# Linear attention and a two-layer MLP on one core: batch 2 projected five groups sooner, its q transposed behind its keys, w_out groups of batch 1's block moved

## The chip, the cores and the metric

The kernel runs on one core of a Trainium2 chip. The metric is device time in microseconds (us) for one execution.

## The reference

For each of 8 batches and 8 heads, keys and values of 1024 tokens are projected to 64 rows, and every query attends to those 64. The result (8192 tokens of 512) goes through two layers with a hard-swish between them.

```python
def _attn_ref(q, k, v, E, F):
    k_proj = np.einsum('ks,bhsd->bhkd', E, k)
    v_proj = np.einsum('ks,bhsd->bhkd', F, v)
    scores = scale * np.matmul(q, k_proj.transpose(0, 1, 3, 2))
    ...                                        # softmax over the 64 projected keys
    return np.matmul(attn, v_proj)

def _moe_ref(x, w_in, w_out):                  # (8192, 512), (512, 2048), (2048, 512)
    h = x @ w_in
    g = h * np.clip(h + 3.0, 0.0, 6.0) / 6.0
    return g @ w_out
```

## The kernel before

The two layers of batch b run while the attention of batch b+1 is fitted in between ("block" below is the loop body of one b). A block has two halves t of 512 tokens; each half has 16 w_in groups (`first_group`, index `fo`). In between stand four `second_group`s, each a quarter of the w_out product of the half before. The stages of the next batch's attention are hung on those w_out groups by the table `plan`.

```python
        if b == 1:
            plan = {4: (4, second.all_scores), 5: (3, second.all_sums), 6: (2, second.first_values),
                    7: (2, lambda: second.some_values((2, 3), ((pmm, pmm), (pmm, pat))))}
        # ... other batches
        for t in range(NB):                    # NB = 2
            g = g_tile()
            for fo in range(FO):               # FO = 16
                # ... the w_in group fo (the first two of a block together)
                pop()                          # one small deferred action, if any
                if b == 1 and t == 0 and fo == 10:
                    second.projected()         # keys and values of batch 2 projected
                if not behind or fo % SB < SB - 1:     # SB = 4: after groups 3, 7, 11, 15
                    continue
                n = t * SB + fo // SB
                if (b, n) == (1, 7):
                    second.first_products()
                when, act = plan.get(n) or (None, None)
                rows = second_group(*behind[0], fo // SB, ...)
                # ... runs in quarters; act() after quarter `when`
            behind = [(b, t, g)]
```

Batch 1 is the first batch that runs in this loop, and `behind` is empty in its first half: its four w_out groups (n = 4 to 7) all stand in the second half, and the whole attention of batch 2 hangs on them. The softmax denominators take a trip through DRAM: ScalarE turns the sums into 16 rows, SyncE writes them to DRAM, and eight transfers, one for each head, read two rows each back to 64 partitions.

```python
        def spread(self, few):
            nc.scalar.activation(few, few, AF.Exp, scale=-1.0)
            rows = dram.tile([H * NB, TOK], f32, tag="rows", name="rows")
            nc.sync.dma_start(out=rows, in_=few[::8])
            # ... recs: four tiles, one for each pair of heads
            for h in range(H):
                (nc.sync, nc.gpsimd)[h % 2].dma_start(out=..., in_=...to_broadcast([D, NB * TOK]))
```

The products `xT = values * rec` (VectorE, two for each pair of heads) make the x that the next block's first w_in group reads. The loads of batch 3 start here, when a tiny GpSimd copy (`mark`) has read what the last transpose wrote:

```python
        def turn(self):
            nc.sync.dma_start_transpose(self.kT, self.kp.rearrange("p h a d -> p (h a d)"))
            last = self.kT[:1, 0, :1]
            if self.b not in (2, 3):
                qT_dma[self.b] = q_transposed(self.b)
                last = qT_dma[self.b][:1, 0, 0, :1]
            if self.b + 1 < B:
                mark = att.tile([1, 1], bf16, tag="mark", name="mark")
                nc.gpsimd.tensor_copy(mark, last)
                load_kqv(self.b + 1, "qkv" if self.b == 2 else "kvq")
```

For batch 2 the transpose of q was issued elsewhere, ahead of batch 1's block and so ahead of the keys' in SyncE's queue.

The softmax here doesn't subtract the row's maximum and nothing guards it: scores larger than these inputs give would overflow.

Of the kernel before, what the change touches and what calls it, by code (L numbers as in the profile page):

```python
# [15 lines left out]
def kernel(  # L16
# [23 lines left out]
    SB = SO // NB  # L40
# [25 lines left out]
    def pmm():  # L66
        return ps_mm.tile([P, TOK], f32, tag="mm", name="mm")
# [5 lines left out]
    def g_tile():  # L73
        return gpool.tile([P, FO, TOK], bf16, tag="g", name="g")
# [48 lines left out]
    def load_kqv(b, order="qkv"):  # L123
        kqv[b] = {}
        for n in order:
            kqv[b][n] = raw_tile(n)
            nc.gpsimd.dma_start(out=kqv[b][n], in_=kqv_dram[n][b])
# [32 lines left out]
    def q_transposed(b):  # L160

        t = qT_pool.tile([P, KO, 2, TOK], bf16, tag="qT", name="qT")
        nc.sync.dma_start_transpose(t.rearrange("p j a (m n) -> p (j a m) n", n=P),
                                    kqv[b]["q"].rearrange("p h s d -> p (h s d)"))
        return t

    qT_dma = {}
# [5 lines left out]
    def in_columns(ps, stationary, moving, **flags):  # L173
        for lo in range(0, stationary.shape[-1], width[0]):
            nc.tensor.matmul(ps[lo:lo + width[0]], stationary[:, lo:lo + width[0]], moving, **flags)  # L175
# [17 lines left out]
    class Attention:  # L193
# [20 lines left out]
            nc.vector.tensor_copy(self.vp[a * KP:(a + 1) * KP], self.ps[KP:].rearrange("p (h d) -> p h d", d=D))  # L214



        def turn(self):
            nc.sync.dma_start_transpose(self.kT, self.kp.rearrange("p h a d -> p (h a d)"))
            last = self.kT[:1, 0, :1]  # L220
            if self.b not in (2, 3):
                qT_dma[self.b] = q_transposed(self.b)
                last = qT_dma[self.b][:1, 0, 0, :1]
            if self.b + 1 < B:
# [3 lines that stand above are left out]
# [285 lines left out]
    def first_group(xT, t, g, fo):  # L513
        h_ps = pmm()
        h_part(h_ps, xT, t, fo, range(KO))
        h_out(h_ps, g, fo)

    def out_rows(b, t, c):
        return out_v[b, :, SB * t + 2 * (c % 2) + c // 2, :]


    def second_group(b, t, g, c, copy=None):
        o_dst = out_rows(b, t, c)
        if (b, t, c) == (B - 1, NB - 1, SB - 1):

            most = d_model * 3 // 4
            for piece, copy, dma in ((slice(0, most), nc.vector.tensor_copy, nc.sync),
                                     (slice(most, d_model), nc.scalar.copy, nc.scalar)):
                n = piece.stop - piece.start
                o_ps = pmm()[:, :n]  # L530
                for fo in range(FO):
                    in_columns(o_ps, g[:, fo, c * P:(c + 1) * P], w_out_sb[:, fo, piece],
                               start=(fo == 0), stop=(fo == FO - 1))
                o_sb = opool.tile([P, d_model], f32, tag="o_sb", name="o_sb")[:, :n]
                copy(o_sb, o_ps)  # L535
                dma.dma_start(out=o_dst[:, piece], in_=o_sb)
            return
        o_ps = pmm()
        for fo in range(FO):
            in_columns(o_ps, g[:, fo, c * P:(c + 1) * P], w_out_sb[:, fo, :],  # L540
                       start=(fo == 0), stop=(fo == FO - 1))
            if fo % SB == SB - 1:
                yield
        o_sb = opool.tile([P, d_model], f32, tag="o_sb", name="o_sb")
        (copy or nc.scalar.copy)(o_sb, o_ps)  # L545
        nc.sync.dma_start(out=o_dst, in_=o_sb)

    def whole(gen):
        for _ in gen:
            pass  # L550

    def x_tile():
        return xpool.tile([P, KO, NB, TOK], bf16, tag="xT", name="xT")
# [42 lines left out]
    behind = []  # L596
# [3 lines left out]
    def pop():  # L600
        if later:
            later.pop(0)()

    rows = [second_group(0, 0, g[0], c) for c in range(SB)]
# [14 lines left out]
    for c in range(SB):  # L619
        for i, _ in enumerate(second_group(0, 1, g[1], c, nc.vector.tensor_copy)):  # L620
# [3 lines left out]
            elif i == 2 or c == SB - 1:  # L624
                while rest:
                    rest.pop()()
    qT_dma[2] = q_transposed(2)
    xT = x_next


# [3 lines left out]
    for b in range(1, B):  # L634
        if b + 1 < B:
            x_next = second.xT = x_tile()
        third = Attention(b + 2) if b + 2 < B else None


        plan = {}  # L640
        two = (pmm, pmm), (pat, pat)
# [3 lines that stand above are left out]
        elif b + 1 < B:  # L645
            plan = {3 + (b == 2): (2, third.projected) if third else None,
                    4 + (b == 2): (2, lambda: second.some_values((0, 1), two)),
                    6: (2, lambda: second.some_values((2, 3), two, third))}
            if b == 2:
                plan.update({0: (2, second.projected), 1: (4, second.all_scores), 2: (4, second.all_sums)})  # L650
            else:
                plan.update({0: (1, lambda: second.some_scores((1, 2, 3), ((pmm, pmm), (pat, pat), (pat, pat)))),
                             1: (4, second.all_sums)})

        for t in range(NB):
            g = g_tile()
            for fo in range(FO):
                if b < 3 and t == 0 and fo < 2:

                    if fo == 0:  # L660
                        TwoGroups(xT, t, g).parts((0, 1, 2), (3,))
                else:
                    first_group(xT, t, g, fo)
                pop()
                if b == 1 and t == 0 and fo == 10:
                    second.projected()
                if not behind or fo % SB < SB - 1:
                    continue
                n = t * SB + fo // SB
                if (b, n) == (1, 7):  # L670
                    second.first_products()
                when, act = plan.get(n) or (None, None)

                rows = second_group(*behind[0], fo // SB,
                                    nc.vector.tensor_copy if second and act == second.all_scores else None)
                for quarter in range(1, SB + 1):
                    next(rows) if quarter < SB else whole(rows)
                    if quarter == when:
                        act()
            behind = [(b, t, g)]  # L680
        if b == 1:
            later.append(lambda: qT_dma.update({3: q_transposed(3)}))
        second, xT = third, x_next
# [32 lines left out]
```

## Time and profile before

| | before |
|---|---|
| time, median (range) of the first 3 runs | 508.66 us (507.2 to 510.09) |
| profiled run: time, span, granted clock | 507.9 us, 505.8 us, 0.999 |
| TensorE busy | 496.9 us (98%) |
| waits of TensorE for x of batch 2 | 1.87 + 0.56 = 2.43 us |

The lines that show this are in the prediction. Two more views are needed for what follows. First the timeline of TensorE and of SyncE's queue around batch 1's block; columns are start in us, duration, engine (PE is TensorE, DVE VectorE, POOL GpSimd, SPq the queue of SyncE), line, operation, output<-input and count; a bracket at the end holds a wait before the line and what ended it. A transfer "lands" when all of its data has arrived; its line in SyncE's queue is over before that (q's transpose below leaves the queue at 97.38 and lands at 99.5). The first line is the start of the block, which is the zero point for comparing profiles, because starts of the program differ by up to 1.5 us between runs (1.3 from before's).

```profile
84.17 9.68 PE L175 MATMUL mm<-xT,w_in_sb 128*32 128x512 bf16 x176
...
92.00 5.38 SPq L163 DMA_TRANSPOSE qT<-q  x1
97.48 1.21 SPq L219 DMA_TRANSPOSE kT<-kp  x1
...
117.52 0.53 SPq L286 DMA_DIRECT2D rows<-few  x1
122.21 2.38 SPq L290 DMA_DIRECT2D rec<-rows  x4
```

The keys' transpose starts at 97.48, right after q's has left the queue, though VectorE had finished its input at 96.94. The rows leave at 117.52 and are back for the broadcasts at 122.2.

Second, busy time by stretches of 1 us; the last three columns are the granted clock of TensorE, the mean busy share of the DMA engines (it can exceed 1: 1.11 in the first line) and GB/s.

```profile
120.00:121.00 1.00, 1.00 (x20) 0.25 (x12) 0.28 (x1) 0.00 (x0) 0.00 (x0) 1.00 1.11 293
...
122.00:123.00 1.00, 1.00 (x24) 0.54 (x20) 0.00 (x0) 0.00 (x0) 0.22 (x1) 1.00 0.02 3
```

Between the end of batch 3's loads and the broadcasts the DMA engines are all but idle for about two microseconds: 3 GB/s in the second line.

### The profile page before, as it was taken

How to read it: one execution, taken by the hardware profiler on the slowest of the kernel's cores; microseconds unless marked ns; L12 is line 12 of the kernel's file. 1: busy time of each engine (PE TensorE's matmuls, PEld its weight loads, DVE VectorE, ACT ScalarE, POOL GpSimd, SP SyncE). 2: the span in 40 equal slices, each digit the busy share in tenths (PEclk: the TensorE clock that was granted, in tenths of full speed). 3: DMA queues.
4: the chain of work that ended last, by engine and by line, in shares of the span. 5: the costliest groups of instructions: out<-in, count | busy, mean ns of one | idle time of the engine just before them, and what ended most of it. 6: DMA issues, size and time to landing. Idle time of an engine off the chain costs nothing.

```text
span 505.8 us, 18693 instructions
## 1 busy us (share of the span) xinstructions
PE 496.9 (98%) x8562; PEld 246.2 (49%) x8562; DVE 245.7 (49%) x384; ACT 244.3 (48%) x425; POOL 51.4 (10%) x82
## 2 busy tenths in 40 slices
PE   8999999999899999999999999999999999999997
PEld 4554554454354444444454544454445444444444
DVE  3572746853744474337533555436552465334420
ACT  3657476565246445633564434652456444443431
POOL 8620020011020120012001020010000100000000
PEclk9999999999999999999999999999999999999999
DMA  9999979799929999469942889257111611101112
GB/s 169 197 205 209 192 146 232 134 161 194 236 53 205 275 148 208 107 189 173 201 100 73 184 156 213 65 138 191 44 43 42 183 55 43 44 23 44 45 44 86
DMA packets 78815, 68.91 MB, mean 136 GB/s; under 512 B 36400, under 2 KB 67376, under 8 KB 78736
## 3 DMA queue, kind: packets, MB, share of 16 engines
q0 software_dynamic: 34400, 35.66, 42.3%
q1 hardware_dynamic: 44112, 31.73, 23.2%
q8 instruction: 67, 1.10, 0.9%
q10 hardware_dynamic: 224, 0.33, 0.3%
q14 instruction: 12, 0.10, 0.1%
HBM read 71.83 MB, written 16.97 MB: 176 GB/s over the span
## 4 chain that ended last, share of the span: by engine, by line
PE 92%; DMA 6%; POOL 1%; issue 1%; ACT 0%; DVE 0%; POOLq 0%; DVEq 0%; ACTq 0%
PE mm L175 85%; PE at L175 2%; DMA rec<-rows 2%; DMA w_in_sb<-in_moe_w_in_dram 2%; DMA k<-in_k_dram 1%; DMA rows<-few 1%; PE mm L254 1%; PE at L236 1%; PE mm L236 1%; PE at L254 1%; PE mm L275 1%; PE at L422 0%; POOL rec L290 0%; POOL q L109 0%; POOL k L113 0%
## 5 line engine op out<-in xcount | busy, mean ns | idle before, releaser
L511 DVE SCALAR_TENSOR_TENSOR g<-r,mm 128x512 bf16<-128x512 f32 x256 | 174.5, 687 | 189.7 <-ACT r L510 189.0
L175 PE MATMUL mm<-w_out_sb,g 128*32 128x512 bf16 (+3 forms) x3904 | 235.9, 376 | 0.0
L175 PE MATMUL mm<-xT,w_in_sb 128*32 128x512 bf16 (+1 forms) x3840 | 231.5, 379 | 2.8 <-DVE xT L267 2.4
L510 ACT ACTIVATE r<-mm 128x512 f32<-128x512 f32 x256 | 153.0, 599 | 74.0 <-PE mm L175 72.0
L175 PEld LDWEIGHTS <-w_in_sb 128*32 128x32 bf16 (+1 forms) x3840 | 110.2, 98 | 113.6 <-issue 4.1
L175 PEld LDWEIGHTS <-g 128*32 128x32 bf16 (+1 forms) x3904 | 109.4, 98 | 111.5 <-issue 6.7
L545 ACT COPY o_sb<-mm 128x512 f32<-128x512 f32 x57 | 33.4, 585 | 146.5 <-PE mm L175 141.5
L290 POOL DMA_DIRECT2D rec<-rows x24 | 12.5, 531 | 194.1 <-DVE g L511 159.3
L245 ACT ACTIVATE aT<-at 128x512 bf16<-128x512 f32 x38 | 21.3, 629 | 7.6 <-PE at L236 7.6
L267 DVE TENSOR_TENSOR xT<-at,rec 128x512 bf16<-128x512 f32 x31 | 19.9, 683 | 6.9 <-ACT rec L187 5.8
L267 DVE TENSOR_TENSOR xT<-mm,rec 128x512 bf16<-128x512 f32 x25 | 16.2, 687 | 6.2 <-PE mm L254 4.9
L211 DVE CAST kp<-at 64x512 bf16<-64x512 f32 x14 | 9.0, 678 | 11.6 <-PE at L175 11.6
L245 ACT ACTIVATE aT<-mm 128x512 bf16<-128x512 f32 x18 | 9.6, 598 | 10.3 <-PE mm L236 10.3
L175 PE MATMUL at<-k,e_t 128*32 128x512 bf16 (+1 forms) x104 | 13.3, 379 | 0.0
L175 PE MATMUL at<-v,f_t 128*32 128x512 bf16 (+1 forms) x104 | 13.2, 379 | 0.0
L214 DVE CAST vp<-at 64x512 bf16<-64x512 f32 x14 | 9.7, 694 | 0.4
L226 POOL COPY mark<-qT 1x1 bf16<-1x1 bf16 x4 | 0.7, 176 | 90.0 <-DMA qT<-q 90.0
L175 PEld LDWEIGHTS <-e_t 128*32 128x32 bf16 (+1 forms) x104 | 5.8, 98 | 5.9
L96 PE MATMUL mm<-ones 128*128 128x512 bf16 x18 | 7.2, 533 | 1.5 <-DVE halves L86 1.5
L535 DVE COPY o_sb<-mm 128x384 f32<-128x384 f32 x1 | 0.6, 558 | 15.2 <-DMA out_dram<-o_sb 15.2
L236 PEld LDWEIGHTS <-kT 64*64 64x64 bf16 x224 | 5.7, 106 | 4.3 <-issue 3.3
L545 DVE COPY o_sb<-mm 128x512 f32<-128x512 f32 x6 | 4.1, 686 | 6.0 <-PE mm L175 6.0
(70 smaller groups left out, 149.6 us busy)
## 6 DMA issues: line engine op xcount, KB each, us to landing
out_dram<-o_sb SPq DMA_DIRECT2D x63, 256.0 KB, 3.7
k<-in_k_dram POOLq DMA_DIRECT2D x7, 1024.0 KB, 11.2
v<-in_v_dram POOLq DMA_DIRECT2D x7, 1024.0 KB, 16.5
q<-in_q_dram POOLq DMA_DIRECT2D x7, 1024.0 KB, 20.8
rec<-rows SPq DMA_DIRECT2D x24, 256.0 KB, 7.0
rec<-rows POOLq DMA_DIRECT2D x24, 256.0 KB, 7.7
w_out_sb<-in_moe_w_out_dram POOLq DMA_DIRECT2D x4, 512.0 KB, 15.9
w_in_sb<-in_moe_w_in_dram POOLq DMA_DIRECT2D x5, 256.0 KB, 9.2
```

The lines of the kernel that those rows point to most:

```text
L96: nc.tensor.matmul(ps, ones[:, :P], ones, start=True, stop=True)
L175: nc.tensor.matmul(ps[lo:lo + width[0]], stationary[:, lo:lo + width[0]], moving, **flags)
L211: nc.vector.tensor_copy(self.kp[:, :, a, :], self.ps[:KP].rearrange("p (h d) -> p h d", d=D))
L214: nc.vector.tensor_copy(self.vp[a * KP:(a + 1) * KP], self.ps[KP:].rearrange("p (h d) -> p h d", d=D))
L236: nc.tensor.matmul(tiles[r][t * KP:(t + 1) * KP, a * HT:(a + 1) * HT], self.kT[r * D:(r + 1) * D, 2 * j + a, :], qT[r * D:(r + 1) * D, j, ...
L245: when(lambda r=r: nc.scalar.activation(aT[:, r].rearrange("p a n -> p (a n)"), tiles[r], AF.Exp, scale=scale))
L254: nc.tensor.matmul(tiles[t][c:c + D].rearrange("p (r n) -> p r n", r=2), stationary(r, 2 * j + a), self.aT[j][r:r + KP, :, a, :], start=Tr ...
L267: when(lambda t=t: nc.vector.tensor_mul(self.xT[:, j, t, :], av[t], rec[:, t]))
L290: (nc.sync, nc.gpsimd)[h % 2].dma_start(out=self.recs[h // 2][h % 2 * D:(h % 2 + 1) * D].rearrange("d t n -> d (t n)"), in_=by_head[h // 4 ...
L510: nc.scalar.activation(r, h_ps, AF.Relu, bias=0.5, scale=1.0 / 6.0)
L511: nc.vector.scalar_tensor_tensor(g[:, fo, :], r, 1.0, h_ps, op0=ALU.min, op1=ALU.mult)
L545: (copy or nc.scalar.copy)(o_sb, o_ps)
```

## The change

The intent: have the reciprocals back in time for the end of batch 1's block. The scores of batch 2 move three w_in groups forward (w_out groups after groups 0, 4, 10, 15 in place of 3, 7, 11, 15), for which the projection moves five groups forward; q's transpose goes behind the keys'.

```diff
         def turn(self):
             nc.sync.dma_start_transpose(self.kT, self.kp.rearrange("p h a d -> p (h a d)"))
             last = self.kT[:1, 0, :1]
-            if self.b not in (2, 3):
+            if self.b != 3:
                 qT_dma[self.b] = q_transposed(self.b)
@@
-    qT_dma[2] = q_transposed(2)
     xT = x_next
@@
+        slots = (0, 4, 10, 15) if b == 1 else (3, 7, 11, 15)
         for t in range(NB):
@@
-                if b == 1 and t == 0 and fo == 10:
+                if b == 1 and t == 0 and fo == 5:
                     second.projected()
-                if not behind or fo % SB < SB - 1:
+                if not behind or fo not in slots:
                     continue
-                n = t * SB + fo // SB
+                n = t * SB + slots.index(fo)
@@
-                rows = second_group(*behind[0], fo // SB,
+                rows = second_group(*behind[0], n % SB,
```

The number of instructions on TensorE is the same in both. I call the three parts "slots", "projection" and "order" below.

## The prediction

> **What bounds the kernel now.** I read the page first, its busy line and the groups of line 175 (the matmul helper).
>
> ```profile
> PE 496.9 (98%) x8562; PEld 246.2 (49%) x8562; DVE 245.7 (49%) x384; ACT 244.3 (48%) x425; POOL 51.4 (10%) x82
> PE 92%; DMA 6%; POOL 1%; issue 1%; ACT 0%; DVE 0%; POOLq 0%; DVEq 0%; ACTq 0%
> L175 PE MATMUL mm<-xT,w_in_sb 128*32 128x512 bf16 (+1 forms) x3840 | 231.5, 379 | 2.8 <-DVE xT L267 2.4
> ```
>
> TensorE is busy for 496.9 of 505.8 us; 8.9 us of the span are without a matmul. The change adds and removes no matmul (the instruction listings of both programs have 17126 TensorE rows), so only those 8.9 us can move. I therefore asked second for every wait of TensorE:
>
> ```profile
> PE mm L175 <- DVE xT L267: 2.4, 2, 1.9
> PE mm L96 <- DVE halves L86: 1.5, 1, 1.5
> PE mm L422 <- ACT aT L442: 0.4, 1, 0.4
> ```
>
> The rest of the 8.9 us lies before the first matmul and after the last. One wait belongs to the part that is changed, the first: two waits, 2.4 us. Third, I looked for its place in the timeline, TensorE and then VectorE from 128 to 138 us, and in the chain that ended last, from 85 to 140 us:
>
> ```profile
> 128.85 1.91 PE L175 MATMUL mm<-w_out_sb,g 128*32 128x512 bf16 x32
> 132.63 1.48 PE L175 MATMUL mm<-xT,w_in_sb 128*32 128x512 bf16 x24 [1.87 <-DVE xT L267]
> 134.67 2.34 PE L175 MATMUL mm<-xT,w_in_sb 128*32 128x512 bf16 x40 [0.56 <-DVE xT L267]
> ```
>
> ```profile
> 130.16 1.29 DVE L267 TENSOR_TENSOR xT<-at,rec 128x512 bf16<-128x512 f32 x2 [1.10 <-DMA rec<-rows]
> 131.88 1.29 DVE L267 TENSOR_TENSOR xT<-mm,rec 128x512 bf16<-128x512 f32 x2 [0.43 <-issue]
> 133.93 0.69 DVE L267 TENSOR_TENSOR xT<-mm,rec 128x512 bf16<-128x512 f32 x1 [0.75 <-DMA rec<-rows]
> ```
>
> ```profile
> 117.52 4.68 DMA rows<-few
> 124.34 9.51 DMA rec<-rows
> 133.93 0.70 DVE xT L267
> ```
>
> At 130.76 us TensorE has finished the w_out groups of batch 1 and wants batch 2's x. The eight products that make it (VectorE, one for each pair of heads and half) wait for the softmax reciprocals, which ScalarE sent to DRAM at 117.52 and eight broadcast transfers bring back; the last lands at 133.85. The batches after it show no such wait. So the whole kernel has 2.43 us (1.87 + 0.56) that this change can take, 0.5% of the time.
>
> **What the Trainium skill says.** "Perfetto Trace Analysis", section "Identifying the Most-Contended Engine", calls matmul busy time a poor measure of roofline and asks for utilization of the peak. The two layers are 4 x 8192 x 512 x 2048 = 34.4 GFLOP; at the page's 78.6 TFLOP/s an estimate of 437 us, 86% of the span: TensorE is really the bound. "DMA: Bandwidth & Descriptors", "Queues, rings and completion order": each DMA engine goes round-robin between the queues that have work. The trace agrees: the 32 KB of rows took 4.68 us beside the loads, against a median of 2.6. "Perfetto Trace Analysis", "Per-instruction lifecycle": the window of a transfer issued by SyncE holds the making of descriptors, not the movement. Here too: q's transpose is 5.38 us on the queue and lands some 7.4 us after its start, so I use landings. "TensorE: Matmul & The Clock Gate", Part 1: idle of about 3.4 us can halve the clock. The wait here is 1.87 us and the granted clock 0.999, so there is no second gain.
>
> **The change part by part.** Durations from the timeline of before: a w_in group (16 matmuls) is 0.865 us (11 groups from 84.17 to 93.68); a w_out group is 3.55 us (103.18 to 106.73); projection 1.73; batch scores 1.21 (106.73 to 107.94).
>
> *Projection after group 5, not 10.* It starts 5 x 0.865 = 4.3 us sooner, at 89.35 for 93.68. Its inputs are there: v of batch 2 was issued at 69.61 and landed 16.7 us later, at 86.3. Slack 3 us, no new wait. VectorE's two casts of the keys end at 92.6 for 96.9.
>
> *q's transpose behind the keys'.* Before, it started at 92.00, as soon as q landed (70.48 + 21.5), and held SyncE to 97.38, so the keys' transpose began at 97.48 and landed at 100.15. Now keys start at about 92.7 and land 2.7 us later; q starts at 92.7 + 1.25 = 93.95 and lands at about 93.95 + 7.4 = 101.35. The scores need it at 104.15 (below): slack 2.8 us.
>
> *Loads of batch 3.* They start when a small GpSimd copy sees the last transpose:
>
> ```profile
> 100.23 0.18 POOL L226 COPY mark<-kT 1x1 bf16<-1x1 bf16 x1 [28.85 <-DMA kT<-kp]
> 100.73 0.88 POOL L127 DMA_DIRECT2D q<-in_q_dram  x1 [0.32 <-issue]
> ```
>
> That copy now waits for q, not for the keys: 101.35 for 100.15. The title says that the loads begin sooner; by my sum they begin about 1.2 us later. I follow the sum, with one chance in three for the title.
>
> *w_out groups after groups 0, 4, 10, 15 for 3, 7, 11, 15.* Only the second half of the block has them. The scores start 3 x 0.865 = 2.6 us sooner (104.15), the sums too (111.4 for 114.0), so the rows leave at 114.9 for 117.52; the first values come 0.9 us sooner. The last slot stays, with the products: x is wanted at 130.76 as before. TensorE's own sum of work is unchanged.
>
> *What reaches the end.* With the same latencies the reciprocals land 2.6 us sooner, the last at 131.25. Two things hold that back. First, VectorE begins the products at 127.78 in both (after the last g of the block), one takes 0.645 us, and TensorE's first matmul follows the fifth (in before it started 0.1 us after it ended): 127.78 + 5 x 0.645 + 0.1 = 131.1, so 0.35 us of waiting stay whatever the transfers do. Greatest gain 2.43 - 0.35 = 2.1 us. Second, the transfers meet the loads. In before the loads were done at about 121.6 (in the windows of 1 us the DMA share falls from 1.11 to 0.58 and 0.02), and the broadcasts ran alone from 124 to 133.4: 9.4 us of DMA work behind 2.4 us of idle DMA. Now rows land at 119.6 and broadcasts start at about 120.5 while loads are still due until 121.6 + 1.2 = 122.8. If the work is only shared out, the last lands near 122.8 + 9.4 = 132.2, plus the half microsecond that landings lag (133.85 against 133.4): 132.7, so 1.1 us sooner, and the third pair near 131.5. Then the fifth product ends at 132.2, TensorE starts at 132.3 (1.5 us of waiting) and the last pair follows in time: gain 0.9 us. Halfway between the two limits, a little toward the second: 1.3 us.
>
> **The rivals.** (1) *The whole wait goes*, gain 2.1 us: if loads begin as early as before or sooner, or the rows land faster than 4.68 us. For it: 2.4 us of idle DMA to fill. (2) *The wait stays*, gain 0 to 0.5: the odd heads' broadcasts are issued by GpSimd, in the same queue as the loads and behind v, and may wait for it to land. Then also the fourth attention product's PSUM tile, free only after the first scaled product, could stop TensorE near 128.5: in before that product started at 127.78 without a wait for its reciprocal, so with little in hand. (3) *A new wait*: q's transpose late for the scores, or PSUM short where scores come behind group 0. Slack of 2.8 us and the same order of tiles speak against both; a stall would cost at most some 2 us, so +1. (4) *TensorE's work itself is faster or slower*: nothing in the diff gives it, and the clock is already 0.999.
>
> **Range and chances.** 508.66 - 1.3 = 507.4 us. Before ran from 507.2 to 510.09 in three runs, so a median of three may be off by about 1 us, more than the rivals differ. From 2.1 us of gain and good runs to a new wait of 1 us with poor ones: 505.5 to 509.4. Two per cent are 10 us, four times all that the change can reach: within 2% nearly certain.
>
> **What would show it.** Right: the wait of line 175 for x falls from 2.4 us to between 0.4 and 1.6; projection at about 89.4; the rows leave at about 114.9; the copy before batch 3's loads runs at about 101.4, no sooner than before; the stretch with 2.4 us of idle DMA near 122 us is gone; the span shortens by 0.9 to 2.1 us and nothing after that wait moves except by it. Wrong in a step: loads that begin before 100 us (the transpose step), broadcasts that still land at 133 or later (rival 2), a wait for scores or PSUM near 100 to 106 us (rival 3). The total would be wrong if the spread of runs exceeds the effect, or if waits appear in later batches.

## The result

| | before | changed |
|---|---|---|
| median (range), 6 runs | 508.38 us (507.12 to 510.09) | 506.74 us (506.16 to 507.15) |
| ratio, 95% interval | | 0.9965 (0.9942 to 0.9988) |
| profiled run: span, granted clock | 505.8 us, 0.999 | 504.9 us, 0.996 |
| TensorE busy | 496.9 us | 498.1 us |

A ratio is the mean time of one kernel's fast runs over that of the other's of the same rounds, so it is not quite the ratio of the medians. A ratio of 0.9965 is 1.8 us less than 508.4 (its interval: 0.6 to 2.9 us less); the medians differ by 1.64. That is within 2%, and faster by more than the noise.

The profile after, first all waits of TensorE (microseconds in total, times, longest):

```profile
PE mm L96 <- DVE halves L86: 1.5, 1, 1.5
PE at L371 <- DMA k<-in_k_dram: 0.5, 2, 0.3
PE mm L414 <- DVE kT L382: 0.3, 1, 0.3
...
```

The wait of line 175 for x, 2.4 us before, is not in the list (its last entry, left out, is 0.3 us too). Then the timeline (lines as before, some shifted by one in the source):

```profile
85.49 5.36 PE L175 MATMUL mm<-xT,w_in_sb 128*32 128x512 bf16 x96
...
94.00 2.46 SPq L218 DMA_TRANSPOSE kT<-kp  x1
96.56 4.06 SPq L163 DMA_TRANSPOSE qT<-q  x1
...
102.34 0.18 POOL L225 COPY mark<-qT 1x1 bf16<-1x1 bf16 x1 [29.70 <-DMA qT<-q]
102.84 0.88 POOL L127 DMA_DIRECT2D q<-in_q_dram  x1 [0.33 <-issue]
...
116.24 0.53 SPq L285 DMA_DIRECT2D rows<-few  x1
121.40 3.05 SPq L289 DMA_DIRECT2D rec<-rows  x4
...
129.09 2.48 DVE L266 TENSOR_TENSOR xT<-at,rec 128x512 bf16<-128x512 f32 x4
...
130.17 1.91 PE L175 MATMUL mm<-w_out_sb,g 128*32 128x512 bf16 x32
131.49 1.88 DVE L266 TENSOR_TENSOR xT<-mm,rec 128x512 bf16<-128x512 f32 x3
132.22 3.64 PE L175 MATMUL mm<-xT,w_in_sb 128*32 128x512 bf16 x64
```

This block began 1.32 us later than in the profile of before (85.49 for 84.17), in a part of the program that the change doesn't touch: in this run the granted clock was 0.66 and 0.78 in two stretches between 15 and 21 us, where it was 1.00 in before. That is why the profiled span is only 0.9 us shorter. Counted from the block's start, the rows leave at 114.92 of before's clock (116.24 - 1.32) and not at 117.52. The eight products run one after the other without a wait for a reciprocal, and TensorE goes on 0.14 us after its last w_out matmul (130.17 + 1.91 = 132.08) where it waited 1.87 and then 0.56 us. Locally the gain is 2.3 us. The DMA engines have no gap before the broadcasts any more, and are nearly done with them within the stretch from 131 us:

```profile
121.00:122.00 1.00, 1.00 (x20) 0.37 (x20) 0.00 (x0) 0.00 (x0) 0.03 (x1) 1.00 1.26 210
...
131.00:132.00 1.00, 1.00 (x20) 0.42 (x13) 1.00 (x2) 0.00 (x0) 0.00 (x0) 1.00 0.63 242
```

But the loads of batch 3 did not begin sooner: 102.84 - 1.32 = 101.52 on before's clock, for 100.73.

### The profile page after: what moved, and what is told of

It reads as the page before. It is cut to its first block, busy times and chain, and to the rows that moved or that the text cites. A ratio compares the mean times of both kernels' runs of the same rounds, so it can differ in the third digit from the quotient of the medians.

```text
span 504.9 us, 18691 instructions
## 1 busy us (share of the span) xinstructions
PE 498.1 (99%) x8562; PEld 247.1 (49%) x8562; DVE 245.5 (49%) x384; ACT 244.5 (48%) x425; POOL 51.5 (10%) x82
## 4 chain that ended last, share of the span: by engine, by line
PE 96%; DMA 1%; DVE 1%; POOL 1%; ACT 1%; issue 0%; ACTq 0%; DVEq 0%; POOLq 0%
PE mm L175 88%; PE at L175 2%; DMA k<-in_k_dram 1%; PE mm L253 1%; PE at L235 1%; PE at L253 1%; PE mm L235 1%; PE at L387 1%; DVE xT L266 1%; PE at L421 1%; PE mm L274 1%; POOL q L109 0%; PE mm L421 0%; PE at L401 0%; POOL k L113 0%
## 5 line engine op out<-in xcount | busy, mean ns | idle before, releaser
L211 DVE CAST kp<-at 64x512 bf16<-64x512 f32 x14 | 9.0, 678 | 11.6 <-PE at L175 11.6
L244 ACT ACTIVATE aT<-mm 128x512 bf16<-128x512 f32 x18 | 9.6, 598 | 10.3 <-PE mm L235 10.3
## 6 DMA issues: line engine op xcount, KB each, us to landing
k<-in_k_dram POOLq DMA_DIRECT2D x7, 1024.0 KB, 11.5
```

The costliest lines, as they stand in the source:

```text
L211: nc.vector.tensor_copy(self.kp[:, :, a, :], self.ps[:KP].rearrange("p (h d) -> p h d", d=D))
L244: when(lambda r=r: nc.scalar.activation(aT[:, r].rearrange("p a n -> p (a n)"), tiles[r], AF.Exp, scale=scale))
```

## The experiments

Theory: the only thing that counts is when the rows leave, that is the slots. Rivals: the earlier projection frees the loads; the order of the transposes counts; loads and broadcasts share a full DMA, so the loads' start decides. The eleven runs in one table. "Waits" are TensorE's waits in the profile for products, scores or x in this stage; each kernel was timed six times (e6 five) against 11 or 12 runs of before on the same chip (e1 to e4 on one, e5 to e11 on another).

| run | what it has | median us | ratio to before (95%) | waits us |
|---|---|---|---|---|
| before | | 508.07 to 508.80 | | 2.4 |
| e1 | slots | 506.24 | 0.9960 (0.9941 to 0.9980) | 0.4 |
| e2 | projection | 507.78 | 0.9982 (0.9967 to 0.9998) | 1.3 + 0.8 |
| e3 | order | 512.50 | 1.0079 (1.0054 to 1.0103) | 3.8 |
| e4 | slots 3, 10, 12, 15 (later sums) | 509.71 | 1.0018 (1.0001 to 1.0035) | 2.5 + 0.3 |
| e5 | order, all broadcasts from SyncE | 511.09 | 1.0057 (1.0038 to 1.0076) | 1.9 + 2.2 |
| e6 | loads of batch 3 at once | 516.44 | 1.0157 (1.0135 to 1.0178) | 8.1 + 0.8 |
| e7 | order + slots | 510.55 | 1.0059 (1.0030 to 1.0087) | 1.4 + 2.9 |
| e8 | full change, loads behind the keys | 507.30 | 0.9982 (0.9963 to 1.0001) | 1.6 |
| e9 | slots + projection | 507.14 | 0.9978 (0.9950 to 1.0006) | 2.0 |
| e10 | order + projection | 508.30 | 1.0000 (0.9978 to 1.0021) | 1.5 |
| e11 | full change again | 506.51 | 0.9971 (0.9950 to 0.9992) | 0.2 |

All were correct.

### e1: the slots alone

The four lines of the diff that deal with `slots`, on before.

> Only the w_out groups of batch 1's block move (after groups 0, 4, 10, 15); projection, transposes and the start of batch 3's loads stay as before. If the rows' earlier departure is the whole cause: projection to block start as before, rows leave 2.6 us sooner than before (counted from the block's start), the wait for x on TensorE falls from 2.4 us to 0.3 or less, time 1.5 to 2.2 us under before, same as the full change. If projecting sooner or the transposes' order is what matters: the wait stays above 1.5 us and the time within 0.7 us of before.

Measured: 506.24 us, ratio 0.9960. On before's clock the rows left at 114.92 (115.30 less 0.38, as the block began at 84.55), and in e1's timeline the wait for x is almost gone:

```profile
115.30 0.52 SPq L286 DMA_DIRECT2D rows<-few  x1
...
131.53 3.64 PE L175 MATMUL mm<-xT,w_in_sb 128*32 128x512 bf16 x64 [0.40 <-DVE xT L267]
```

The slots alone give what the full change gives (0.9965 and, again, 0.9971). The wait was 0.1 us more than expected.

### e2: the projection alone

```diff
-                if b == 1 and t == 0 and fo == 10:
+                if b == 1 and t == 0 and fo == 5:
```

> Only the projection moves (after group 5); q's transpose stays ahead of the keys', slots stay. The keys' transpose is stuck behind q's on SyncE (q lands at 92 us and its transpose holds the queue to 97.4), so it should not start sooner and batch 3's loads should begin within 0.3 us of before's 100.7; wait for x 2.0 to 2.8 us, time within 0.7 us of before. Rival, projection frees the loads: loads begin 3 us or more sooner, the wait falls under 1 us.

The timeline of e2, SyncE's queue and GpSimd:

```profile
98.03 1.22 SPq L219 DMA_TRANSPOSE kT<-kp  x1
...
101.26 0.88 POOL L127 DMA_DIRECT2D q<-in_q_dram  x1 [0.32 <-issue]
```

As expected, the keys' transpose still stands behind q's in the queue (q's held it from 92.50 to 97.93), and the loads begin nearly when they did (101.26, with this run's block 0.15 us later: 0.4 us after before's, where 0.3 was allowed). The waits add up to 2.1 us, near before's 2.4, but 1.3 of them stand at another place: at a values product that needs a PSUM tile (a buffer for matmul results) which the first scaled product frees. So which reciprocal is late differs from profile to profile even with the same transfers. The time is 0.9 us under before by the ratio, a little more than expected, with an interval that just excludes none. e9 against e1 (0.9 us slower with the projection than without, on another chip) says the opposite, so I don't count it as an effect of the projection; it stays open.

### e3: the order alone

```diff
-            if self.b not in (2, 3):
+            if self.b != 3:
@@
-    qT_dma[2] = q_transposed(2)
```

> Only the transposes' order: q's transpose of batch 2 behind its keys', projection still after group 10, slots as before. Batch 3's loads should begin some 5 us later than before (near 105.5 us) and still run when the broadcasts of the reciprocals start. Theory A, broadcasts lose little to loads beside them: wait for x 2.0 to 3.0 us, time within 0.7 us of before. Theory B, loads and broadcasts share a full DMA (the prediction's step): last broadcast some 2.6 us later, wait 4.5 to 5.5 us, time 2 to 3 us over before. Theory C, the odd heads' broadcasts sit behind v in GpSimd's queue: like B in time, but SyncE's broadcasts land as in before.

Measured: 512.5 us, 3.7 us over before's 508.8, and more than any theory said. GpSimd, VectorE and TensorE in the timeline:

```profile
107.86 0.90 POOL L127 DMA_DIRECT2D v<-in_v_dram  x1
...
131.87 1.29 DVE L267 TENSOR_TENSOR xT<-at,rec 128x512 bf16<-128x512 f32 x2 [3.93 <-DMA rec<-rows]
132.62 0.40 PE L254 MATMUL at<-aT,vp 64*64 64x512 bf16 x2 [3.76 <-DVE xT L267]
132.95 2.96 PE L175 MATMUL mm<-w_out_sb,g 128*32 128x512 bf16 x32
```

And one stretch of 1 us of e3, with the granted clock third from the end:

```profile
134.00:135.00 1.00, 1.00 (x16) 0.48 (x12) 1.00 (x2) 0.00 (x0) 0.00 (x0) 0.50 0.07 27
```

Three things stand here. The loads began 5.3 us later, as computed. The first pair's reciprocal came 3.9 us late, and TensorE stopped not at x but earlier, at a values product whose PSUM tile is free only after the first scaled product: the place that the prediction's rival 2 names. And after 3.76 us without a matmul the granted clock fell to one half for some 3.4 us (0.83, 0.50, 0.50, 0.50 and 0.97 in the stretches from 133 us): the same 32 w_out matmuls took 2.96 us for 1.91. So the wait is paid twice. The six runs fall in two groups by their clock, 510.92 to 511.79 us at 0.996 and 0.997, 513.22 to 514.89 us at 0.993.

Of the theories none fits as it stands. The DMA engines' traffic ended at about 133.5, nearly as in before (133.3), but the last broadcast landed at 135.7 on before's clock for 133.85, so 1.8 us later where B has 2.6. SyncE's own broadcasts landed 0.8 to 2.4 us later too, which C does not have. What TensorE waited for is the first pair: of its two broadcasts SyncE's landed at 128.33 and GpSimd's, queued behind v (landed at 130.39), at 131.85.

### e4: the sums three groups later

```diff
-        slots = (0, 4, 10, 15) if b == 1 else (3, 7, 11, 15)
+        slots = (3, 10, 12, 15) if b == 1 else (3, 7, 11, 15)
```

The rest as in e1.

> Before with slots 3, 10, 12, 15: the sums, and so the rows, leave three groups (2.6 us) later than before, near 120.1 us. Theory A1, the rows' departure carries one to one to the end: wait for x 4.5 to 5.5 us, time 2.6 us over before. Theory A2, before's rows lost 2 us to the loads (4.7 us to landing for a median of 2.6): the rows leave when the loads are nearly done and land 2.6 us later, so only some 0.5 to 1 us is lost: wait 2.9 to 3.5 us.

SyncE's queue in e4:

```profile
120.36 0.53 SPq L286 DMA_DIRECT2D rows<-few  x1
123.33 2.39 SPq L290 DMA_DIRECT2D rec<-rows  x4
```

The rows left 2.6 us later than before (120.36 less 0.26 is 120.10, for 117.52), but the broadcasts could start only 0.9 us later (123.07 for 122.21): the rows came back in 3.0 us for 4.7, because the loads were nearly over. The time is 0.9 us over before. A2 is right, at the lower end of its range (2.9 us of waits): while the loads run, sending the rows 2.6 us later costs a third of that.

### e5: e3 with every broadcast of batch 2 from SyncE

```diff
-                (nc.sync, nc.gpsimd)[h % 2].dma_start(...)
+                (nc.sync, nc.sync if self.b == 2 else nc.gpsimd)[h % 2].dma_start(...)
```

(and the diff of e3)

> As e3 (q's transpose behind the keys' alone, which cost 3.7 to 4 us because the first products waited 3.9 us for a reciprocal), but all eight broadcasts of batch 2 are issued by SyncE, none by GpSimd behind the loads. Theory C (the odd heads' broadcasts wait in GpSimd's queue for v of batch 3, which landed at 130.4 us, 1.5 us before the first product could start): the first product starts by 129 us, TensorE's waits for products fall from 3.8 us to 2.5 or less, time at most 1.5 us over before. Theory B (the DMA engines are shared by bytes, whoever issues): waits and time as in e3, within 1 us of it.

The timeline, then one stretch of 1 us:

```profile
129.72 1.29 DVE L267 TENSOR_TENSOR xT<-at,rec 128x512 bf16<-128x512 f32 x2 [2.05 <-DMA rec<-rows]
...
130.79 3.15 PE L175 MATMUL mm<-w_out_sb,g 128*32 128x512 bf16 x32
...
135.40 1.89 DVE L267 TENSOR_TENSOR xT<-mm,rec 128x512 bf16<-128x512 f32 x3 [2.14 <-DMA rec<-rows]
```

```profile
132.00:133.00 1.00, 1.00 (x16) 0.48 (x12) 1.00 (x2) 0.00 (x0) 0.00 (x0) 0.50 0.97 242
```

Neither theory alone. The first product starts 1.9 us sooner than in e3, counted from the block's start (129.72 + 0.19 for 131.87 - 0.08): so much of its delay was GpSimd's queue, where head 1's broadcast stands behind v. But eight broadcasts from one queue beside the loads end later (the last landed at 136.24 for e3's 135.76): the third pair came 2.1 us late, and the waits are 4.1 us in all. Queue order and sharing both count. And a wait of 1.88 us was followed this time by half the clock for about 3.4 us, with 3.15 us for the 32 matmuls; waits of 1.87 us in the profile of before, 2.03 in e9 and 2.04 in e4 were not, so the length of the wait alone does not decide it.

### e6: the loads of batch 3 at once

```diff
-                mark = att.tile([1, 1], bf16, tag="mark", name="mark")
-                nc.gpsimd.tensor_copy(mark, last)
+                if self.b != 2:
+                    mark = att.tile([1, 1], bf16, tag="mark", name="mark")
+                    nc.gpsimd.tensor_copy(mark, last)
```

> Before, but batch 3's loads follow batch 2's at once (no copy that waits for the keys' transpose), so that they are done near 113 us, ahead of the rows at 117.5. If before's wait came from the loads (rows 4.7 us to landing): rows land in 3 us or less, broadcasts start near 120.5, the wait for x falls from 2.4 us to 0.5 or less, time 1.5 to 2.2 us under before, as the full change. If not the loads but the broadcasts' own 9.4 us bind: wait above 1.2 us. Side effect to watch: q's transpose of batch 2 runs beside the loads and may land after 106.7 us, when the scores want it.

The timeline of e6, SyncE's queue and TensorE:

```profile
92.43 19.73 SPq L163 DMA_TRANSPOSE qT<-q  x1
...
115.05 0.64 PE L237 MATMUL mm<-qT,kT 64*64 64x256 bf16 x8 [8.09 <-DMA kT<-kp]
```

The side effect ate the experiment: q's transpose beside the loads took 22.0 us to land in place of 7.5, the keys' stood behind it, and TensorE waited 8.1 us for the scores (and then ran at half clock). One thing is still read from it: with no loads left the rows landed in 1.8 us. It does not say what before would do without the loads.

### e7: the change without its earlier projection

The diff of e3 and the slots of e1.

> The change without its earlier projection (slots 0, 4, 10, 15 and q behind keys; projection after group 10). q's transpose should land near 105.4 us while the scores follow group 0 at about 104.2: TensorE waits about 1.2 us there. Loads begin near 105.6 and v of batch 3 lands near 130, so by theory C the odd broadcasts come late: first product waits to about 131, as in e3. Time 2 to 4 us over before, 4 to 6 over the full change. If the slots alone give the gain whatever the loads do: time 0.5 us over the full change or less.

TensorE in the timeline of e7:

```profile
133.74 0.63 PE L254 MATMUL at<-aT,vp 64*64 64x512 bf16 x2 [2.86 <-DVE xT L267]
```

Both waits came as computed: 1.41 us at the scores for q's transpose (1.2 expected), then the late first reciprocal as in e3, in the line above (the first product at 132.3 on before's clock, for 131 expected). The median is 4.0 us over the full change's 506.51. Projecting sooner gains nothing by itself, but it is what the new order needs.

### e8: the full change with the loads started by the keys' transpose

```diff
-                last = qT_dma[self.b][:1, 0, 0, :1]
+                last = last if self.b == 2 else qT_dma[self.b][:1, 0, 0, :1]
```

> The full change, with batch 3's loads started when the keys' transpose lands (near 96 us) and not q's: loads some 4 to 5 us sooner, so that they do begin sooner than before. The wait for x is down to 0.15 us in the full change, so no gain is left: time within 0.7 us of the full change (1.0 to 2.3 us under before). Rival: q's transpose beside the loads lands after 104.2 us and the scores wait: time above the full change by that wait.

TensorE in the timeline of e8:

```profile
106.47 0.41 PE L235 MATMUL mm<-qT,kT 64*64 64x256 bf16 x8 [1.60 <-DMA qT<-q]
```

Now the loads do begin sooner, at 97.58 (the first one's issue), and it is no gain: q's transpose beside them took 10.3 us to land and the scores waited 1.6 us. The time is 507.3 us, 0.8 over the full change on the same chip (e11) by the medians. The rival in the expectation was right.

### e9, e10, e11: the remaining combinations

e9 is the slots of e1 with the projection of e2; e10 the diffs of e2 and e3 together, without the slots; e11 the whole diff.

> Slots and earlier projection, q's transpose still ahead of the keys' (the change without its reordering). e1 says the slots alone remove the wait for x, so nothing is left: wait 0.5 us or less, time within 0.7 us of e1 and of the full change. If e2's 0.8 us for projecting sooner is real and separate, time 0.6 us or more under e1 (505.6 or less).

TensorE in the timeline of e9:

```profile
132.85 3.64 PE L175 MATMUL mm<-xT,w_in_sb 128*32 128x512 bf16 x64 [2.03 <-DVE xT L267]
```

and the four broadcasts of SyncE's queue, first in e1, then in e9:

```profile
120.37 2.38 SPq L290 DMA_DIRECT2D rec<-rows  x4
120.29 3.58 SPq L290 DMA_DIRECT2D rec<-rows  x4
```

A miss: the rows left at 114.93 on before's clock, and yet the third pair's reciprocal came 1.8 us late and the wait is 2.0 us. The six runs spread from 505.85 to 509.92 us. The loads began as in before and the broadcasts 1.98 us sooner than in before, and e1 sends the same transfers in the same order. The trace shows which one was slow: SyncE's third broadcast (head 4) held the queue for 1.78 us where e1's took 0.58, and landed 10.5 us after its issue for 8.2, at 131.98. GpSimd's of the same pair had landed at 129.58. e6 has the same (1.77 us on the queue, 10.2 to landing) with no loads beside the broadcasts, so the loads are not needed for it; why it happens stays open. The fastest run of e9, 505.85 us, is as fast as e1's (505.82).

> Reordering and earlier projection with the old slots (the change without the slots). Rows leave at 117.5 as before, loads begin about 0.8 us later than before and not 5 us as in e3. If the slots carry the gain: waits for products of 2 to 3.5 us remain, time within 1 us of before. If earlier projection carries it: wait under 1 us, time as the full change.

Measured 508.3 us, as before; the wait is 1.5 us, under the 2 to 3.5 expected. Without the slots there is no gain.

> The full change itself, on the same chip as e9 and e10, to compare them directly and to see the spread of its runs: 506.2 to 507.2 us, 1.3 to 2.2 us under before, the wait for x 0.5 us or less, and no granted clock under 0.995 in any run. If before's spread of 3 us is the size of its wait, the spread of this one is about half of before's or less.

Measured 506.51 us with five runs from 506.13 to 507.28 and one of 508.64; wait 0.17 us, granted clock 0.997 or more in all runs. The spread is 2.5 us for before's 3.2 on this chip, so the expectation that it halves is not met in this set (in the first six runs it was 1.0 us for 3.0). That the length of the wait makes before's spread is therefore not shown.

**What follows from the table.** Medians of different chips can't be set side by side to some tenths (before itself has 508.07 and 508.80), so go by the ratios. The slots alone (e1) and the full change, measured twice, have 0.9960 to 0.9971; order and projection without the slots (e10) have 1.0000. The slots are the gain. In between, and not told apart by these runs, lie e9 (0.9978, interval up to 1.0006), e8 and e2 (both 0.9982). Order and projection together neither add nor take (full change against e1), order alone costs 4 us. No experiment points to a version that would be faster than e1 or the full change: with 0.2 to 0.4 us of wait in their profiles, this place has little more to give, unless slow broadcasts like e9's also occur in their slower runs, which no profile shows.

## Why the prediction was right

The measured median, 506.74 us, lies in the range (505.5 to 509.4), and the forecast of 1.3 us gained stands against 1.6 by the medians and 1.8 by the ratio. The total is a weak test: 1.3 was set between two limits, 0.9 and 2.1, and the measured interval of 0.6 to 2.9 us holds both. The traces tell them apart, and they show the upper limit. By its steps, with times on before's clock (less 1.32 us in the first profile of the change, less 0.33 in e11):

- **The bound and the most to be had: right.** One wait of 2.43 us; 2.3 us of it went, and no other wait of TensorE moved by more than 0.3 us. (The list of waits in before has three more, of 0.3, 0.3 and 0.2 us, which the prediction put before the first matmul and after the last; it changes nothing.)
- **q's transpose and the loads: right in sign, a little too large.** The copy was expected at 101.35 for before's 100.23 and ran at 101.02 (e11: 100.52). So the loads begin 0.8 us later (e11: 0.3), not 1.2, and not sooner, as the title that came with the change had it. Projection started at 89.36, for 89.35 expected. The first profile's keys' transpose held the queue for 2.46 us and not 1.25, but q's then landed after 5.7 us and not 7.4.
- **The rows: right.** Expected at 114.9, measured 114.92 and 114.93. They took 5.1 us to land and not 4.68, so they were back at 120.1, for 119.6 expected; the broadcasts followed at once, for 120.5 expected.
- **The floor set by VectorE: right, smaller.** 0.35 us expected, 0.14 and 0.17 measured; the first four products took 0.62 us each and not 0.645.
- **The size of the sharing: the failed term.** The prediction put "122.8 + 9.4 = 132.2" for the end of the broadcasts, as if all of their 9.4 us of traffic had to follow the end of the loads, and so 132.7 for the last landing; without any sharing it had 131.25. The last broadcast landed at 131.2 (e11: 131.1). TensorE waited 0.14 and 0.17 us, under the 0.4 to 1.6 that the prediction named as its own sign of being right: the outcome was the first rival, the whole wait gone. From the first broadcast's issue to the last landing it took 11.2 and 11.0 us in the two profiles of the change and 11.4 in e1, whose broadcasts run beside the last 3 to 4 us of the loads; it took 11.6 in before, 11.5 in e4 and 10.5 in e8, where the loads are over or within half a microsecond of it (e9, discussed below, took 12.3). So the tail of the loads cost nothing that can be told from this spread. That 9.4 us of busy engines were not 9.4 us of work for the broadcasts is seen in before's timeline: they hold also a store of the output and the start of batch 3's q transpose (131.94), which now come after the broadcasts. Whether that is all of it stays open. In e9, which sends its rows as early, 2.0 us of the wait stayed: the outcome of the second rival, but not by its way, because the late broadcast was SyncE's and not one of GpSimd's behind v.
- **Rival 2's place was real.** e3, e5 and e7 stop TensorE at the values product for want of a PSUM tile (e2 and e4 too, for 1.3 and 0.35 us), and e5 shows 1.9 us of e3's delay to be GpSimd's queue. In the full change it did not happen: v landed there at 123.8, GpSimd's first broadcast at 127.0.
- **"No second gain" from the clock: right for before** (0.998 or more in all of its runs on both chips of the experiments), but not with certainty: e5 lost the clock after a wait of 1.88 us, while e4 and e9 kept it through 2.04 and 2.03.

## What to carry to other kernels

When the busiest engine stands at 98%, list its waits and move the producer of the one that is left; the parts of the change that don't advance that producer are worth nothing, and one of them cost 4 us until another paid for it. A small transfer that has to come back before work can go on should leave while it can still be late: here 2.6 us sooner was worth 1.8 us, and 2.6 us later cost only 0.9, because it then no longer had to share with the loads (4.7 us to landing beside them, 3.0 near their end). Before a bulk load is started sooner, look which small transfer or transpose it will run beside: that one may be the one that is waited for.

## What the Trainium skill lacked or had wrong

- "TensorE: Matmul & The Clock Gate", Part 1, gives an idle window of about 3.4 us as what brings the half clock. e5 had it after 1.88 us without a matmul (granted clock 0.50, 32 matmuls in 3.15 us for 1.91), e7 after 2.86 us, while 1.87 us in before, 2.03 in e9 and 2.04 in e4 passed at 1.00. So waits shorter than the window can cost the clock, and their length alone does not say which do.
- "DMA: Bandwidth & Descriptors", section "Rules for kernel authors", says that a transpose next to ordinary DMAs needs nothing. That speaks of correctness; no page has its time beside loads. The 1 MB transpose of batch 2's q landed in 5.6 to 7.6 us without loads beside it, in 10.3 us beside them (e8) and in 22.0 us where the loads were queued ahead of it (e6).
- The same page, "Queues, rings and completion order", has the round-robin between queues and, of the queues of SyncE and ScalarE, the ring order within one; e3 shows such an order in GpSimd's queue as well (e3 against e5: 1.9 us for a broadcast behind v). No page has the time of a small transfer beside loads: 32 KB of rows took 4.7 us to land beside loads, 3.0 near their end (e4) and 1.8 without (e6).
